# Pooled attention and two gated products on one core: probabilities transposed over 128 partitions, their blocks moved by transfers inside SBUF

## The chip, the cores and the metric

The kernel runs on one core of a Trainium2 chip. The metric is the device time of one execution in microseconds (us). Three runs of the kernel before took 1653.54, 1659.47 and 1664.84 us; their median is 1659.47 us. The engines are PE (TensorE), DVE (VectorE), ACT (ScalarE), POOL (GpSimd) and SP (SyncE, which here only issues transfers). All inputs are float32 arrays of the reference's shapes, except that the weights are held as 8-byte floats and are turned into 4-byte ones on the chip.

## The reference

```python
def _attn_ref(q, k, v):                       # B=8, H=8, S=576, D=64
    k_p = k.reshape(B, H, 72, 8, D).mean(axis=3)      # pooled by 8: 72 keys
    v_p = v.reshape(B, H, 72, 8, D).mean(axis=3)
    scores = np.matmul(q, k_p.transpose(0, 1, 3, 2)) / np.sqrt(D)
    scores = scores - np.max(scores, axis=-1, keepdims=True)
    attn = np.exp(scores)
    attn = attn / (np.sum(attn, axis=-1, keepdims=True) + 1e-09)
    return np.matmul(attn, v_p)

def _moe_ref(x, w1, w2, w3, w_out):           # x: 4608 x 512, d_ff 1024
    return ((x @ w1) * (x @ w2) @ w3) @ w_out

def _moe2_ref(x, w_gate, w_val, w_out, rms_g):    # d_ff 1536
    xn = x / np.sqrt(np.mean(x * x, axis=-1, keepdims=True) + 1e-06) * rms_g
    g = xn @ w_gate
    return (g * (1 / (1 + np.exp(-g))) * (xn @ w_val)) @ w_out
```

The attention's output of all heads, 512 columns for each of 4608 tokens, goes through the first product and then the second.

## The kernel before

The 4608 tokens are taken in nine blocks of 512 (`NB`), which do not fall together with the eight batches of 576. Matmuls are done on fp32r tiles split into a high and a low part, three matmuls for each product (`mm3`, lines 103 to 106), so that the times in the trace for lines L104, L105 and L106 are the kernel's main work.

The program has five stages:

1. Setup. w3 times w_out is formed on PE (L626), the weights w1 and w2 are converted (`Conv`), and batch 0 goes through attention.
2. The attention stage. For each block i, `ab(i, m, s)` (L564) makes one 128 x 512 piece of x @ w1 (s = 0) or x @ w2 (s = 1) in 12 matmuls, and their product h is stored to device memory (L575). Between these calls stand the steps of the next batch's attention, by a table of 16 positions for a block, `positions(i)` (L796): a position is the place after one `ab`.
3. The second stage, `second` (L489), multiplies the stored h, loaded again (`h_load`, L1185), with the formed w3 @ w_out. The result y of a block goes to device memory, and its mean square is formed on the way (`y_end`, L654: squares L659, the split L673, two matmuls with a column of ones L681 and L682, then small transfers L685, L687 and L692).
4. Block 0 of the second product (`gv`, L967).
5. The other eight blocks of it in pairs (`quad`, L1066).

The weights of stages 4 and 5 are prepared in twelve groups by `gv_steps` (L717): converted, combined by subtractions (L745), split (L100 on ACT, L101 on DVE) and stored by POOL (L762). Four groups are spread over stage 2 (`prep`), and eight, together with the conversion of the last weight w_o2 (`o2_jobs`, L861), over the end of stage 2 and the whole of stage 3 (`side`).

One batch's attention has five tiles of queries, four of 128 rows and one of 64. The steps of tile t are: `Q` (q is transposed on PE, L307, and copied by ACT, L312), `S` (scores on PE L325, row maximum on DVE L337, exponentials on ACT L340), `N` (division on DVE, L351 to L353), and `T` (the probabilities, rows = queries, are transposed so that rows = pooled keys, into the tile aT). For batches 0 and 1 `T` uses PE (L375) and ACT (L380). From batch 2 on it uses DVE's transpose of 32 x 32 blocks, each instruction on 32 partitions, straight into aT:

```python
for i in range(2 * hf, min(2 * hf + 2, n // 32)):
    for kb in range(SPP // 32):
        nc.vector.transpose(
            aT[32 * kb : 32 * kb + 32, :, s0 + 32 * i : s0 + 32 * i + 32],
            s_t[t][32 * i : 32 * i + 32, :, 32 * kb : 32 * kb + 32],
        )
```

`av_step` (L420) multiplies aT with the pooled v on PE (L428); ACT (L435) and DVE (L436) take the result out of PSUM as the high and low part of the next block's input. The first of `k0`, `k1`, `kT` load and pool k for the next batch (L247 from SP, L248 added by POOL) and transpose it on PE (L288).

A scheduler records each engine's instructions in one order, in which the engine runs them. Every transfer issued by SP or ACT counts its landing on one of eight semaphores (they are called DMAHW0 to DMAHW7), given out in turn, and waits before its issue for the landing of the transfer that had the same semaphore before it.

The attention's PSUM tiles (`pa`, `apsum`, L74) are four banks used in turn; a fifth use waits until the first has been read by ACT and DVE.

Of the kernel before, what the change touches and what calls it, by code (L numbers as in the profile page):

```python
# [21 lines left out]
def kernel(  # L22
# [17 lines left out]
    nc = tc.nc  # L40
# [223 lines left out]
    def att_steps(b):  # L264
        q_t, qT_t, s_t, mx_t, den_t, kv_t = {}, {}, {}, {}, {}, {}

        def load_q(g):
            if 2 * g >= NTL:
                return
            q_t[g] = at_p.tile([P, 2, H, D], F32, tag="q", name="q", bufs=2)  # L270
            for u, (s0, n) in enumerate(TILES[2 * g : 2 * g + 2]):
                nc.sync.dma_start(
                    out=q_t[g][:n, u], in_=q[b, :, s0 : s0 + n, :].rearrange("h s d -> s h d")
                )

# [18 lines left out]

        def step_Q(g, hf):
            if 2 * g >= NTL:
                return
            tiles = TILES[2 * g : 2 * g + 2]
            nu, n = len(tiles), tiles[0][1]
            qt = q_t[g].rearrange("s u h d -> s u (h d)")  # L300
            if hf == 0:
                qT_t[g] = at_p.tile([P, 2, NP, P], F32, tag="qT", name="qT", bufs=2)
            qT = qT_t[g]
            if hf < nu:
                ps = apsum()
                for p in range(NP):
                    nc.tensor.transpose(  # L307
                        ps[:, p * P : p * P + n],
                        qt[:n, hf, p * P : (p + 1) * P],
                        ident[:n, :n],  # L310
                    )
                nc.scalar.copy(  # L312
                    qT[:, hf, :, :n], ps.rearrange("d (p s) -> d p s", p=NP)[:, :, :n]
                )
            if hf == 1:
                q_t.pop(g)
                load_q(g + 2)

        def step_S(t, hf):
            s0, n = TILES[t]  # L320
            ps = apsum()
            if hf == 0:
                s_t[t] = sbuf[t % len(sbuf)]
            for p in (2 * hf, 2 * hf + 1):
                nc.tensor.matmul(  # L325
                    ps[:n, (p % 2) * 2 * SP : (p % 2 + 1) * 2 * SP],
                    qT_t[t // 2][:, t % 2, p, :n],
                    kT[:, p, :],
                    start=True,
                    stop=True,  # L330
                )
# [28 lines left out]
        def step_T(t, hf):  # L360
            s0, n = TILES[t]
            if t == 0 and hf == 0:
                st8["aT", b] = at_p.tile([SPP, H, S], F32, tag="aT", name="aT")
            aT = st8["aT", b]
            if b >= 2:
                for i in range(2 * hf, min(2 * hf + 2, n // 32)):
                    for kb in range(SPP // 32):
                        nc.vector.transpose(  # L368
                            aT[32 * kb : 32 * kb + 32, :, s0 + 32 * i : s0 + 32 * i + 32],
                            s_t[t][32 * i : 32 * i + 32, :, 32 * kb : 32 * kb + 32],  # L370
                        )
# [7 lines left out]
            dst = aT[:SP, 4 * hf : 4 * hf + 4, s0 : s0 + n]  # L379
            nc.scalar.copy(dst, src)  # L380

# [10 lines left out]
        def flat():  # L392
            steps = [step_kT, lambda: step_Q(0, 0), lambda: step_Q(0, 1)]
            for t in range(NTL):
# [6 lines left out]
                def e(t=t):  # L401
# [4 lines left out]
                    lambda t=t: step_S(t, 0),  # L406
                    lambda t=t: step_Q(t // 2 + 1, t % 2),
                    lambda t=t: step_S(t, 1),
                    d,
                    e,  # L410
# [4 lines left out]
        return SimpleNamespace(  # L415
            flat=flat, k0=step_k0, k1=step_k1, q=load_q, kT=step_kT, Q=step_Q,
            S=step_S, N=step_N, T=step_T, load_v=load_v, v=step_v,
        )

    def av_step(b, i, p):  # L420
# [143 lines left out]
    def ab(i, m, s):  # L564
# [152 lines left out]
    def gv_steps(G, s, kp):  # L717
        w = (w_gate, w_val)[s]
        cell = {}

        late = G > 0

# [64 lines left out]
    for n, (cs, steps) in enumerate(groups):  # L787
        gv_prep = preps[n >= 4]
        if n in (0, 4):
            gv_prep.append(lambda cs=cs: [cs_.s0() for cs_ in cs])  # L790
        if n + 1 not in (4, len(groups)):
            nxt = groups[n + 1][0]
            steps[4] = lambda f=steps[4], nxt=nxt: (nxt[0].s0(), nxt[1].s0(), f())
        gv_prep += steps

    def positions(i):  # L796
        pos = [[] for _ in range(2 * KF1)]
        b = i + 1
        if b >= B:
            return pos  # L800
        A = atts[b]
        pos[1] = av_steps(i, i + 1) + [
            lambda: A.S(0, 0), lambda: A.Q(1, 0), lambda: A.S(0, 1)
        ]
        pos[2] = [lambda: A.N(0)]
        for t in range(1, NTL):
            p = 2 * t + 1
            pos[p] += [lambda t=t: A.S(t, 0)]
            if t < 4:
                pos[p] += [lambda t=t: A.Q(1 + t // 2, t % 2)]  # L810
            pos[p] += [lambda t=t: A.S(t, 1)]
            pos[p + 1] += [
# [3 lines left out]
        pos[12] += [lambda: A.T(NTL - 1, 0), lambda: A.T(NTL - 1, 1)]  # L816
        pos[13] += av_steps(b, i + 1)
        if b + 1 < B:
# [4 lines left out]
            pos[11] += [C.k1, lambda: C.q(1)]  # L823
            pos[15] += [C.kT, lambda: C.Q(0, 0), lambda: C.Q(0, 1)]
        return pos
# [5 lines left out]
    pos = positions(0)  # L831
    pos[0] += [atts[1].kT, lambda: atts[1].Q(0, 0), lambda: atts[1].Q(0, 1)]
    half = [pos[2 * n] + pos[2 * n + 1] for n in range(KF1)]
# [504 lines left out]
```

## Time and profile before

| | us |
|---|---|
| median of three runs | 1659.47 |
| the profiled execution | 1663.74 |
| its span (first to last instruction) | 1662.0 |
| PE busy in the span | 1609.1 (97%) |
| DVE busy | 1018.0 (61%) |
| ACT busy | 680.1 (41%) |
| POOL busy | 93.1 (6%) |

A matmul's busy time overlaps that of the next one: a 128 x 512 matmul is shown as 389 ns long, while the next one starts some 227 ns after it. So PE's rate is read from counts in a stretch, and its losses from idle time and from the granted clock. The clock column is the share of full speed (2.4 GHz) that was granted; 0.5 is the lower of the two levels, 1.2 GHz. Times on the time axis are us from the start of the span.

### The profile page before, as it was taken

To read this page: it belongs to the slowest core of one execution; us is meant where nothing else is said; L and a number is where in the kernel's file an instruction comes from. 1 tells how busy PE (TensorE), PEld (TensorE's weight loads), DVE (VectorE), ACT (ScalarE), POOL (GpSimd) and SP (SyncE) were. 2 spreads that over 40 slices of the span, in tenths; PEclk is the share of its full clock that TensorE was granted. 3 is DMA by queue.
4 is the path that set the end of the run, shared out by engine and by line. 5 is a ranking of instruction groups with operands and counts; after the bars stand their busy time and mean duration, and the time that the engine had idled before them with its cause. 6 is when DMAs were issued, how large, how long until landed. Compare 5 with 4: busy or idle time off the path is not lost. (4 is left out here: it accounts for less than half of the span.)

```text
span 1662.0 us, 19939 instructions
## 1 busy us (share of the span) xinstructions
PE 1609.1 (97%) x7250; PEld 1281.7 (77%) x7250; DVE 1018.0 (61%) x1773; ACT 680.1 (41%) x1607; POOL 93.1 (6%) x107
## 2 busy tenths in 40 slices
PE   5899999999999999999899999999999999999999
PEld 2447778778777788888678888888888888888887
DVE  4677598779787147766736353485347635475444
ACT  4765635543453125555523233244323433233321
POOL 1001101110110011111000000000000000000000
PEclk9898999999999999999999999999999999999999
DMA  9858445664562178887887754467445735455422
GB/s 229 258 163 221 106 119 154 140 150 111 145 215 84 70 242 297 268 281 244 314 289 242 294 212 176 154 206 275 158 158 210 284 138 217 177 207 198 177 102 76
DMA packets 147462, 322.53 MB, mean 194 GB/s; under 512 B 52506, under 2 KB 79130, under 8 KB 129443
## 3 DMA queue, kind: packets, MB, share of 16 engines
q1 hardware_dynamic: 126210, 276.13, 49.2%
q0 software_dynamic: 21152, 45.12, 10.4%
q8 instruction: 57, 0.93, 0.2%
q14 instruction: 43, 0.34, 0.1%
HBM read 247.75 MB, written 73.44 MB: 193 GB/s over the span
## 5 line engine op out<-in xcount | busy, mean ns | idle before, releaser
L104 PE MATMUL ps<-xf,wr 128*128 128x512 f32 x576 | 224.1, 389 | 0.0
L106 PE MATMUL ps<-xf,wr 128*128 128x512 f32 x576 | 224.1, 389 | 0.0
L105 PE MATMUL ps<-xf,wr 128*128 128x512 f32 x576 | 224.1, 389 | 0.0
L105 PE MATMUL o<-ol,hch 128*128 128x512 f32 x384 | 149.4, 389 | 0.0
L104 PE MATMUL o<-oh,hch 128*128 128x512 f32 x384 | 149.4, 389 | 0.0
L106 PE MATMUL o<-oh,hcl 128*128 128x512 f32 x384 | 149.4, 389 | 0.0
L368 DVE STREAM_TRANSPOSE aT<-s 32x256 f32<-32x256 f32 x324 | 140.9, 435 | 5.2
L1081 ACT COPY f<-ps 128x512 f32<-128x512 f32 x144 | 84.4, 586 | 126.1 <-PE ps L106 121.3
L104 PEld LDWEIGHTS ps<-xf,wr 128*128 128x128 f32 x576 | 108.1, 188 | 22.6 <-ACT f L1081 0.2
L105 PEld LDWEIGHTS ps<-xf,wr 128*128 128x128 f32 x576 | 108.1, 188 | 22.4
L106 PEld LDWEIGHTS ps<-xf,wr 128*128 128x128 f32 x576 | 108.1, 188 | 22.4
L1085 DVE TENSOR_TENSOR f<-y,f 128x512 f32<-128x512 f32 x48 | 33.2, 691 | 149.9 <-PE y L106 149.9
L104 PE MATMUL ps<-xh,w1h 128*128 128x512 f32 x288 | 119.3, 414 | 0.0
L340 ACT ACTIVATE s<-pa,mx 128x72 f32<-128x72 f32 (+1 forms) x280 | 85.5, 332 | 73.8 <-DVE mx L337 73.7
L105 PE MATMUL ps<-xl,w1h 128*128 128x512 f32 x288 | 114.9, 399 | 0.0
L104 PE MATMUL ps<-xh,w2h 128*128 128x512 f32 x288 | 113.1, 393 | 1.8 <-ACT w2h L100 1.8
L106 PE MATMUL ps<-xh,w1l 128*128 128x512 f32 x288 | 113.7, 395 | 0.0
L106 PE MATMUL ps<-xh,w2l 128*128 128x512 f32 x288 | 112.4, 390 | 0.0
L105 PE MATMUL ps<-xl,w2h 128*128 128x512 f32 x288 | 112.4, 390 | 0.0
L1105 ACT CAST hch<-f 128x512 fp32r<-128x512 f32 x72 | 44.8, 623 | 105.0 <-DVE f L1099 105.0
L1167 DVE TENSOR_TENSOR acc<-o,acc 128x512 f32<-128x512 f32 x64 | 43.5, 687 | 68.1 <-PE o L106 68.1
L626 PE MATMUL wps<-wo,hl 128*128 128x512 f32 x128 | 68.9, 664 | 16.6 <-ACT hl L559 9.6
(198 smaller groups left out, 3253.9 us busy)
## 6 DMA issues: line engine op xcount, KB each, us to landing
wr<-wd SPq DMA_DIRECT2D x96, 1024.0 KB
wd<-wst POOLq DMA_DIRECT2D x48, 512.0 KB, 6.1
hr<-hd SPq DMA_DIRECT2D x36, 512.0 KB
oh<-od SPq DMA_DIRECT2D x15, 1024.0 KB
ol<-od SPq DMA_DIRECT2D x15, 1024.0 KB
wr<-wd SPq DMA_DIRECT2D x24, 512.0 KB
x1raw<-in_moe_w_dram SPq DMA_DIRECT2D x20, 512.0 KB
hd<-hh SPq DMA_DIRECT2D x40, 256.0 KB
```

Source lines behind the costliest of these rows:

```text
L104: nc.tensor.matmul(o, lh, rh, start=first, stop=False, skip_group_check=part)
L105: nc.tensor.matmul(o, lh, rl, start=False, stop=False, skip_group_check=part)
L106: nc.tensor.matmul(o, ll, rh, start=False, stop=last, skip_group_check=part)
L340: nc.scalar.activation(s_t[t][:n, h, :SP], pv[:, j, :], AF.Exp, bias=mx[:, j, :], accum_out=den_t[t][:n, h, :],)
L368: nc.vector.transpose(aT[32 * kb : 32 * kb + 32, :, s0 + 32 * i : s0 + 32 * i + 32], s_t[t][32 * i : 32 * i + 32, :, 32 * kb : 32 * kb + 32],)
L626: nc.tensor.matmul(wps[i], wt[:, i * P : (i + 1) * P], wo[j // 4][:, j % 4, :], start=j == 0, stop=j == KF1 - 1,)
L1081: nc.scalar.copy(t, bank)
L1085: nc.vector.tensor_tensor(out=t, in0=bank, in1=t, op=ALU.add)
L1105: nc.scalar.copy(hi, hf)
L1167: nc.vector.tensor_tensor(out=a, in0=ys[j], in1=a, op=ALU.add)
```

## The change

`T` of batches 2 to 7 becomes two parts. DVE transposes all partitions of a tile of queries at once, three instructions for a tile, into a new tile tT (two buffers); then SP issues transfers from SBUF to SBUF, one for each 32 x 32 block row, twelve for a tile of 128 queries and six for the tile of 64, which bring the blocks from the partitions of the queries to those of the keys in aT. aT is laid out anew, with 32 columns of a head side by side and the heads 32 columns apart, so `av_step` reads its operand in pieces of 32 columns, and ACT's copy of batches 0 and 1 (`T` on PE) writes in that layout.

q is loaded tile by tile into three buffers, and its transposes stand behind both halves of the scores instead of between them. h is stored from ACT's queue instead of SP's. Eight of the twelve weight groups instead of four are spread over stage 2. `av_steps` stands one position later.

```diff
-        def load_q(g):
-            if 2 * g >= NTL:
+        def load_q(t):
+            if t >= NTL:
                 return
-            q_t[g] = at_p.tile([P, 2, H, D], F32, tag="q", name="q", bufs=2)
-            for u, (s0, n) in enumerate(TILES[2 * g : 2 * g + 2]):
-                nc.sync.dma_start(
-                    out=q_t[g][:n, u], in_=q[b, :, s0 : s0 + n, :].rearrange("h s d -> s h d")
-                )
+            s0, n = TILES[t]
+            q_t[t] = at_p.tile([P, H, D], F32, tag="q", name="q", bufs=3)
+            nc.sync.dma_start(
+                out=q_t[t][:n], in_=q[b, :, s0 : s0 + n, :].rearrange("h s d -> s h d")
+            )
...
+            nc.scalar.copy(
+                qT_t[t][:, :, :n], ps.rearrange("d (p s) -> d p s", p=NP)[:, :, :n]
+            )
+            load_q(t + 3)
...
         def step_T(t, hf):
             s0, n = TILES[t]
+            g0, ng = s0 // 32, n // 32
             if t == 0 and hf == 0:
-                st8["aT", b] = at_p.tile([SPP, H, S], F32, tag="aT", name="aT")
+                st8["aT", b] = at_p.tile([SP, S // 32, H, 32], F32, tag="aT", name="aT")
             aT = st8["aT", b]
             if b >= 2:
-                for i in range(2 * hf, min(2 * hf + 2, n // 32)):
-                    for kb in range(SPP // 32):
-                        nc.vector.transpose(
-                            aT[32 * kb : 32 * kb + 32, :, s0 + 32 * i : s0 + 32 * i + 32],
-                            s_t[t][32 * i : 32 * i + 32, :, 32 * kb : 32 * kb + 32],
+                if hf:
+                    return
+                tT = at_p.tile([P, SPP // 32, H, 32], F32, tag="tT", name="tT", bufs=2)
+                for kb in range(SPP // 32):
+                    nc.vector.transpose(
+                        tT[:n, kb], s_t[t][:n, :, 32 * kb : 32 * kb + 32]
+                    )
+                for kb in range(SPP // 32):
+                    r = min(32, SP - 32 * kb)
+                    for i in range(ng):
+                        nc.sync.dma_start(
+                            out=aT[32 * kb : 32 * kb + r, g0 + i],
+                            in_=tT[32 * i : 32 * i + r, kb],
                         )
                 return
...
-                st8["aT", b][:SP, h, c0 : c0 + n],
+                st8["aT", b][:, c0 // 32 : (c0 + n) // 32, h, :],
...
-            h_put.append(lambda: nc.sync.dma_start(out=hdram[i][m], in_=hf))
+            h_put.append(lambda: nc.scalar.dma_start(out=hdram[i][m], in_=hf))
...
-        late = G > 0
+        late = G > 1
...
-        gv_prep = preps[n >= 4]
-        if n in (0, 4):
+        gv_prep = preps[n >= 8]
+        if n in (0, 8):
...
-            lambda: A.S(0, 0), lambda: A.Q(1, 0), lambda: A.S(0, 1)
+            lambda: A.S(0, 0), lambda: A.S(0, 1), lambda: A.Q(1)
...
-        pos[13] += av_steps(b, i + 1)
+        pos[14] += av_steps(b, i + 1)
```

What the scheduler makes of it is shown at three places. A name is a tile, `_121` and the like a buffer's number, `x3` three in a row.

The first place is DVE at the end of a block, from the last tile but one of the batch to the step that empties the banks `pa` of `av_step` (aT and tT: the transposes; den and s: the division; kv and vp: the pooling of k and v; xl: the banks being emptied). Before:

```order
L337 TENSOR_REDUCE mx<-pa 64x4
L368 STREAM_TRANSPOSE aT<-s_121 32x8x32 x11
L351 TENSOR_SCALAR den<-den 64x8
L574 TENSOR_TENSOR hh<-ps,f 128x512
L352 RECIPROCAL den<-den 64x8
L253 TENSOR_TENSOR kv<-kv 72x4x128
L353 TENSOR_TENSOR s_120<-s_120,den 64x8x72
...
L368 STREAM_TRANSPOSE aT<-s_120 32x8x32 x6
L574 TENSOR_TENSOR hl<-ps,f 128x512
L436 SCALAR_TENSOR_TENSOR xl_3173<-pa,xh_3172 128x192 x4
```

Of the change:

```order
L333 TENSOR_REDUCE mx<-pa 64x4 x2
L367 STREAM_TRANSPOSE tT<-s_121 128x256 x2
...
L349 TENSOR_TENSOR s_120<-s_120,den 64x8x72
L367 STREAM_TRANSPOSE tT<-s_120 64x256 x2
L581 TENSOR_TENSOR hh<-ps,f 128x512
...
L367 STREAM_TRANSPOSE tT<-s_120 64x256
...
L581 TENSOR_TENSOR hl<-ps,f 128x512
L443 SCALAR_TENSOR_TENSOR xl_3307<-pa,xh_3306 128x192
...
L443 SCALAR_TENSOR_TENSOR xl_3307<-pa,xh_3306 128x192 x3
```

Between the last maximum and the emptying of the banks 17 transposes of 32 partitions stood; now five of 128 or 64 partitions stand there.

The second place is SP's queue at two tiles of a batch in stage 2 (hd: h in device memory; in brackets the semaphores waited for). Before:

```order
L575 DMA hd_98<-hl 128x512 [waits DMAHW6_49,DVE_49]
L272 DMA q<-in_q_dram 128x8x64 [waits DMAHW7_49,PE_49]
L575 DMA hd_98<-hh 128x512 [waits DMAHW0_49,DVE_49]
L272 DMA q<-in_q_dram 128x8x64 [waits DMAHW1_49]
L272 DMA q<-in_q_dram 128x8x64 [waits DMAHW3_49,DMAHW2_49,PE_49]
L575 DMA hd_98<-hl 128x512 [waits DVE_49]
```

Of the change:

```order
L272 DMA q<-in_q_dram 128x8x64 [waits DMAHW1_49,PE_49]
L373 DMA aT<-tT 32x256 [waits DMAHW2_49,DVE_49]
L373 DMA aT<-tT 32x256 [waits DMAHW3_49]
L373 DMA aT<-tT 32x256 [waits DMAHW5_49]
L373 DMA aT<-tT 32x256 [waits DMAHW6_49]
L373 DMA aT<-tT 32x256 [waits DMAHW7_49,DVE_49]
L373 DMA aT<-tT 32x256 [waits DMAHW0_49]
L373 DMA aT<-tT 32x256 [waits DMAHW1_49]
L373 DMA aT<-tT 32x256 [waits DMAHW2_49]
L373 DMA aT<-tT 8x256 [waits DMAHW3_49,DVE_49]
L373 DMA aT<-tT 8x256 [waits DMAHW4_49]
L373 DMA aT<-tT 8x256 [waits DMAHW5_49]
```

The stores of h have left SP's queue, and the blocks of aT stand in it; from the eighth on each of them waits for the landing of one of the same tile. DMAHW4 is missing among the first because a store of h on ACT has it there.

The third place is ACT at the end of stage 3 (xq: w_o2 being converted; hb: h being split; of: w_o2 being split; `f<-y` and `hh<-y`: y of the last block but one; the last row is the split of its sum of squares, L673 before and L680 now). Before:

```order
L662 COPY hh<-y 128x512
L659 ACTIVATE f<-y 128x512 x2
L662 COPY hh<-y 128x512
L100 CAST hb<-hr 128x1024
L144 ACTIVATE xq<-xq 128x512
L147 ACTIVATE f<-xq 128x512
L673 CAST f<-f 128x512
```

Of the change:

```order
L669 COPY hh<-y 128x512
L666 ACTIVATE f<-y 128x512
L100 CAST hb<-hr 128x1024
L666 ACTIVATE f<-y 128x512
L669 COPY hh<-y 128x512
L100 CAST of<-of 128x2048
L680 CAST f<-f 128x512
```

The conversion step that stood in front of the split has moved; the split of a finished group of w_o2 stands there instead.

## Rows read from the trace of the kernel before

**Rows 1.** Busy time of each engine by stage (setup, attention, second stage, its end).

```profile
core 0: us, PE busy (x) PEld busy (x) DVE busy (x) ACT busy (x) POOL busy (x), PEclk, DMA share, GB/s
0.00:160.00 160.00, 128.01 (x471) 74.02 (x472) 99.41 (x192) 94.69 (x235) 15.64 (x22) 0.92 0.82 222
160.00:540.00 380.00, 374.02 (x1928) 298.55 (x1927) 314.57 (x710) 178.39 (x746) 38.55 (x38) 0.99 0.52 136
540.00:780.00 240.00, 240.00 (x1055) 194.54 (x1054) 136.40 (x200) 107.48 (x156) 30.77 (x37) 1.00 0.71 237
780.00:860.00 80.00, 68.83 (x282) 54.25 (x282) 46.84 (x67) 36.35 (x54) 7.10 (x9) 0.94 0.88 303
```

**Rows 2.** What PE waited for: us in total, times, longest us.

```profile
PE pa L288 <- DVE xl L436: 6.0, 4, 2.6
PE y L681 <- ACT f L673: 4.6, 1, 4.6
...
PE y L104 <- ACT f L684: 3.0, 1, 3.0
```

**Rows 3.** DVE from 197 to 540 us: busy, mean ns | idle before.

```profile
L368 DVE STREAM_TRANSPOSE aT<-s 32x256 f32<-32x256 f32 x324 | 140.9, 435 | 5.2
...
L353 DVE TENSOR_TENSOR s<-s,den 128x576 f32<-128x576 f32 x24 | 18.2, 757 | 0.7
...
L101 DVE TENSOR_TENSOR wst<-wf,wst 128x1024 fp32r<-128x1024 f32 x8 | 9.7, 1220 | 2.4 <-ACT wst L100 2.4
L745 DVE TENSOR_TENSOR wf<-wf 128x256 f32<-128x256 f32 x16 | 6.1, 417 | 0.1
L159 DVE SCALAR_TENSOR_TENSOR rawp<-rawp 128x512 int32<-128x512 int32 x8 | 5.5, 684 | 0.1
L171 DVE CUSTOM_DVE_ANT_0 wf<-rawp,f 128x1024 uint16<-128x1024 uint16 x8 | 5.4, 672 | 0.1
...
L353 DVE TENSOR_TENSOR s<-s,den 64x576 f32<-64x576 f32 x6 | 4.5, 748 | 0.1
...
L168 DVE TENSOR_SCALAR f<-f 128x512 int32<-128x512 int32 x8 | 3.4, 419 | 4.5 <-ACT f L147 4.5
```

**Rows 4.** DVE in order of time at one block's end: start, us.

```profile
415.45 2.67 DVE L368 STREAM_TRANSPOSE aT<-s 32x256 f32<-32x256 f32 x6
...
418.75 1.14 DVE L436 SCALAR_TENSOR_TENSOR xl<-pa,xh 128x192 fp32r<-128x192 f32 x4
```

**Rows 5.** PE in order of time at the same place.

```profile
419.16 0.47 PE L288 MATMUL pa<-ident,kv 72*128 72x72 f32 x4 [2.62 <-DVE xl L436]
```

**Rows 6.** Granted clock (third number from the right) behind two of PE's waits.

```profile
420.00:424.00 4.00, 4.00 (x14) 3.31 (x13) 2.76 (x3) 1.55 (x4) 1.98 (x3) 0.57 0.72 201
...
804.00:808.00 4.00, 3.38 (x8) 2.29 (x9) 3.41 (x5) 1.38 (x2) 0.00 (x0) 0.50 0.91 295
```

**Rows 7.** ACT in order of time at the end of the second stage.

```profile
802.72 0.65 ACT L144 ACTIVATE xq<-xq 128x512 int32<-128x512 uint32 x1 [3.01 <-DMA xq<-in_moe_w_out_dram]
...
803.83 0.61 ACT L673 CAST f<-f 128x512 fp32r<-128x512 f32 x1
```

**Rows 8.** What SP's queue waited for: us in total, times, longest us.

```profile
SPq L575 <- DVE hh L574: 127.7, 23, 10.6
...
SPq L687 <- DMA sdram<-f: 15.2, 7, 5.7
```

**Rows 9.** SP in order of time: a load of 288 KB, and a store of 2 KB.

```profile
404.02 0.35 SPq L247 DMA_DIRECT2D kv<-in_v_dram  x1
...
835.77 0.24 SPq L685 DMA_DIRECT2D sdram<-f  x1
...
844.50 0.32 SPq L687 DMA_DIRECT2D ss<-sdram  x1
```

**Rows 10.** POOL in order of time: the addition that waits for that load.

```profile
409.21 1.18 POOL L248 DMA_DIRECT2D kv<-in_v_dram  x1 [1.47 <-DMA kv<-in_v_dram]
```

**Rows 11.** The attention's last product on PE, the whole span: busy, mean ns.

```profile
L428 PE MATMUL pa<-aT,vp 72*64 72x64 f32 (+7 forms) x240 | 32.6, 406 | 2.7 <-ACT kT L293 2.7
```

More of the change, by code (lines that the diff above doesn't have):

```diff
@@ L265, in att_steps, with load_q3 @@
         q_t, qT_t, s_t, mx_t, den_t, kv_t = {}, {}, {}, {}, {}, {}
-        def load_q(g):
-            if 2 * g >= NTL:
+        def load_q(t):
+            if t >= NTL:
                 return
-            q_t[g] = at_p.tile([P, 2, H, D], F32, tag="q", name="q", bufs=2)
-            for u, (s0, n) in enumerate(TILES[2 * g : 2 * g + 2]):
-                nc.sync.dma_start(
-                    out=q_t[g][:n, u], in_=q[b, :, s0 : s0 + n, :].rearrange("h s d -> s h d")
-                )
+            s0, n = TILES[t]
[3 more added lines that the diff above has]
+            )
+        def load_q3(g):
+            for t in ((0, 1), (2,))[g]:
+                load_q(t)
         def step_k0():
@@ L293, in step_kT, with step_Q @@
             nc.scalar.activation(kT[D:, :, SP:], pv[D:], AF.Copy, scale=ATT_SCALE)
-        def step_Q(g, hf):
-            if 2 * g >= NTL:
+        def step_Q(t):
+            if t >= NTL:
                 return
[L298 to L313, printed above, removed]
-                )
-            if hf == 1:
-                q_t.pop(g)
-                load_q(g + 2)
+            n = TILES[t][1]
+            qt = q_t.pop(t).rearrange("s h d -> s (h d)")
+            qT_t[t] = at_p.tile([P, NP, P], F32, tag="qT", name="qT", bufs=2)
+            ps = apsum()
+            for p in range(NP):
+                nc.tensor.transpose(
+                    ps[:, p * P : p * P + n], qt[:n, p * P : (p + 1) * P], ident[:n, :n]
+                )
+            nc.scalar.copy(
+                qT_t[t][:, :, :n], ps.rearrange("d (p s) -> d p s", p=NP)[:, :, :n]
+            )
+            load_q(t + 3)
         def step_S(t, hf):
@@ L326, in step_S @@
                     ps[:n, (p % 2) * 2 * SP : (p % 2 + 1) * 2 * SP],
-                    qT_t[t // 2][:, t % 2, p, :n],
+                    qT_t[t][:, p, :n],
                     kT[:, p, :],
@@ L378, in step_T @@
             src = ps[:SP].rearrange("s (h t) -> s h t", h=4)[:, :, :n]
-            dst = aT[:SP, 4 * hf : 4 * hf + 4, s0 : s0 + n]
-            nc.scalar.copy(dst, src)
+            nc.scalar.copy(
+                aT[:, g0 : g0 + ng, 4 * hf : 4 * hf + 4, :],
+                src.rearrange("s h (g c) -> s g h c", c=32),
+            )
         def load_v():
@@ L392, in flat @@
         def flat():
-            steps = [step_kT, lambda: step_Q(0, 0), lambda: step_Q(0, 1)]
+            steps = [step_kT, lambda: step_Q(0)]
             for t in range(NTL):
@@ L406, in flat @@
                     lambda t=t: step_S(t, 0),
-                    lambda t=t: step_Q(t // 2 + 1, t % 2),
                     lambda t=t: step_S(t, 1),
+                    lambda t=t: step_Q(t + 1),
                     d,
@@ L415, in att_steps @@
         return SimpleNamespace(
-            flat=flat, k0=step_k0, k1=step_k1, q=load_q, kT=step_kT, Q=step_Q,
+            flat=flat, k0=step_k0, k1=step_k1, q=load_q3, kT=step_kT, Q=step_Q,
             S=step_S, N=step_N, T=step_T, load_v=load_v, v=step_v,
@@ L787 @@
     for n, (cs, steps) in enumerate(groups):
-        gv_prep = preps[n >= 4]
-        if n in (0, 4):
+        gv_prep = preps[n >= 8]
+        if n in (0, 8):
             gv_prep.append(lambda cs=cs: [cs_.s0() for cs_ in cs])
-        if n + 1 not in (4, len(groups)):
+        if n + 1 not in (8, len(groups)):
             nxt = groups[n + 1][0]
@@ L807, in positions @@
             p = 2 * t + 1
[L808 to L811, printed above, removed]
+            pos[p] += [lambda t=t: A.S(t, 0), lambda t=t: A.S(t, 1), lambda t=t: A.Q(t + 1)]
             pos[p + 1] += [
@@ L823, in positions @@
             pos[11] += [C.k1, lambda: C.q(1)]
-            pos[15] += [C.kT, lambda: C.Q(0, 0), lambda: C.Q(0, 1)]
+            pos[15] += [C.kT, lambda: C.Q(0)]
         return pos
@@ L831 @@
     pos = positions(0)
-    pos[0] += [atts[1].kT, lambda: atts[1].Q(0, 0), lambda: atts[1].Q(0, 1)]
+    pos[0] += [atts[1].kT, lambda: atts[1].Q(0)]
     half = [pos[2 * n] + pos[2 * n + 1] for n in range(KF1)]
```

## The prediction

> **What bounds the kernel now.** I began with busy time by stage. In the attention stage PE is busy 374.0 of 380 us, in the second stage all of it, at the end of the second stage 68.8 of 80, in the setup 128.0 of 160 [rows 1]. So PE is the bound, and a change can gain only what PE loses: 6.0 us of idle in the attention stage, 11.2 at the end of the second stage, 32 in the setup, and what the lower clock takes there (0.99, 0.94, 0.92 of full speed).
>
> Next, whom PE waits for. In the attention stage it is one wait: L288, the transposes of k at a block's end, stands four times, 6.0 us in all, for L436 on DVE, which empties the PSUM banks that L288 needs [rows 2]. DVE in order of time shows why L436 is late: six transposes stand before it until 418.1, it begins at 418.75, and PE goes on at 419.16 after 2.62 us of idle [rows 4, 5]. DVE is behind because of its load: its transposes are 324 times 435 ns, 140.9 us [rows 3]. Behind that wait the granted clock reads 0.57, the lower level for most of 4 us, after 1.00 before it [rows 6].
>
> At the end of the second stage PE waits 4.6 us for L673 and 3.0 us for L684, both on ACT [rows 2]. ACT is not busy there: at 802.72 it ends an idle time of 3.01 us with a conversion step whose load of w_o2 came late, and L673 stands in the queue behind it [rows 7]. The transfer engines are 0.88 busy in that stage, against 0.52 in the attention stage [rows 1].
>
> **The change, part by part.** *Transposes.* 324 become 90: three for each of five tiles of six batches. The price on 128 partitions isn't in the trace. From below it is 435 ns, the same 256 elements a partition; from above 4 x 435 = 1740 ns, if the four groups of 32 partitions went one after another. I take 435: L353 takes 757 ns on 128 partitions and 748 on 64, so DVE's time goes by elements per partition [rows 3]. DVE loses 234 x 435 = 101.8 us.
>
> The Trainium skill, "VectorE: DVE Perf Modes", section "The three transpose paths", has a 128 x 128 bf16 transpose done as a grid of independent 32 x 32 blocks in 311 ns. By it a 128 x 256 one would take about 622 ns, an estimate, and the loss would be 140.9 - 90 x 0.622 = 84.9 us, which leaves the sum as it is.
>
> *Weight groups.* Four more groups in the attention stage cost DVE 2 x (0.684 + 0.672 + 0.419 + 1.220) + 4 x 0.417 = 7.7 us each [rows 3], 30.7 in all. DVE's 314.6 us in that stage [rows 1] become 314.6 - 101.8 + 30.7 = 243.5, or 64% of 380 instead of 83%. Their loads and stores come along, 3 MB a group, 12 MB over 380 us, 32 GB/s beside 136 [rows 1].
>
> *The wait of L288.* Seventeen transposes stood between the last maximum and the emptying of the banks, 17 x 0.435 = 7.4 us; five stand there now, 2.2 us. The longest wait is 2.6 us [rows 2], so it should go, though `av_steps` moves one position nearer (12 matmuls, 12 x 240 / 1055 = 2.7 us, [rows 1]). That is 5.2 us less of DVE work against 2.7 us less of cover, a net 2.5 us at the longest wait, and DVE no longer arrives there late. Gain 6.0 us, and about 2 us of clock (4 us at 0.57 lose 1.7, the shorter waits a little): 8 us. From below the gain is nothing, if DVE still comes late.
>
> *Blocks of aT by transfer.* 324 new transfers, 54 a batch, at about 0.33 us of SP's time (0.35 and 0.32 for two others, [rows 9]): 18 us a block of some 57. They hide as long as aT is full when `av_step` comes. The last tile's are issued after position 12 and used after position 1 of the next block, five positions or 13.6 us later. A landing isn't in the trace for this size. From below it is 2.2 us, the mean of SP's wait for a 2 KB store (15.2 / 7, [rows 8]); from above 8.5, the one time that this store met full transfer engines (835.77 + 0.24 to 844.50, [rows 9]). The kv load in the attention stage landed within 5.2 us (404.02 to 409.21, [rows 9, 10]). I take 3, since 32 KB is nearer to the small store in the stage's half-idle engines. With eight semaphores a tile's last four wait for its first landings: 3 + 4 x 0.35 + 3 = 7.4 us after the first issue, inside 13.6. Cost 0.
>
> The Trainium skill, "DMA: Bandwidth & Descriptors", section "Anatomy of one DMA", speaks against many small transfers: each costs about 2 us whatever its size. One after another that would be 54 x 2 = 108 us a block, an estimate, and SP would bound the stage; eight at once it is 13.5 us. No row before shows which.
>
> *h from ACT's queue.* Eight stores a block leave SP, which stood 127.7 us for one of their kinds alone [rows 8]; q, k and v behind them go sooner, which nothing waits for. ACT gets 8 x 0.33 = 2.7 us a block and is 178.4 of 380 busy [rows 1]. A store there waits for a product that DVE made one `ab` earlier, and for its semaphore's last landing, usually a block of aT one tile before. Behind it stand the copies and exponentials; PE has three further banks, so I cost it at nothing. Without that cover each us of waiting is one of PE's.
>
> *Reading aT in pieces of 32 columns.* L428 is 32.6 us [rows 11]; no strided operand of PE stands in the trace. Between 0 and 32.6 I take 0: the pieces are contiguous and the count of columns is the same.
>
> *Order of q's transposes; the layout of ACT's copy; the setup.* The same instructions in another order; q's third and fourth loads wait for PE in SP's queue, one of them more than before. The setup loses 32 us [rows 1] in waits of single us, and I take 0 with 5 either way.
>
> *The end of the second stage.* `side` loses 32 of its 79 steps, so the steps of w_o2 (the last 14, with 12 loads of 512 KB and 6 stores of 1 MB) spread over some 25 of its 82 calls instead of 15. The conversion step in front of L673 is gone from ACT's queue there, and loads arrive sooner. I take the 4.6 us, a third of the 3.0, and 1.7 of clock (half of the 3.38 us that PE is busy at 0.50, [rows 6]): 7 us. From below 0 (the split of w_o2 that now stands ahead may be as late), from above all 11.2.
>
> **The sum.** 8 + 7 = 15 us off the profiled execution's 1663.74 gives 1648.7. That execution lies 4.3 above the median of the three runs; taking the gain from the median gives 1644.5. I say **1648**.
>
> **The rivals.** *Both gains, as forecast: 0.45*, 1640 to 1656. *Only the attention stage gains: 0.22.* For it: at the second stage's end PE also waits behind the chain of small transfers (L685, L687), which the change leaves in place [rows 9]. 1663.7 - 8 = 1655.7. *More than forecast: 0.13.* SP, freed of h, feeds the setup's last loads and the whole 11.2 us go: 1663.7 - 8 - 11.2 - 5 = 1639.5, down to 1630.
>
> *SP's queue takes the place of DVE, slower: 0.12.* A tile comes every two `ab`, 5.5 us plus its small matmuls, about 6.8. If a landing takes L, a full tile's twelve transfers hold SP for L + 1.4 us, and its q load 0.5 more. Over the four full tiles the delay is 4 x (L + 1.9 - 6.8), against a margin of 13.6 - L - 6 x 0.35 for the last tile's six. They meet at L = 6.2 us; above it `av_step` waits. At L = 7 the delay is 8.4 and the margin 4.5: 3.9 us a block and 1.7 of clock, six blocks, 34 us, so 1663.7 - 15 + 34 = 1683. For it: 8.5 us was seen, the kv load took 5.2. Against it: this stage's engines are at 0.52, and h has left the queue.
>
> *PE reads aT at half rate: 0.04.* 1648.7 + 32.6 = 1681. *The transposes cost fourfold, so DVE isn't relieved: 0.04.* 314.6 + 90 x 1.74 - 140.9 + 30.7 = 361 of 380: the waits at L288 stay or double, 1663.7 - 7 + 6 = 1663.
>
> **Range and chances.** 1% of the median is 16.6 us, about what a measurement of this kernel can tell from no change: below 1642.9 is faster, above 1676 slower. The forecast's lower part (0.17 of its 0.45, since from the median the same gain gives 1644.5) and 0.13 of more make faster 0.30; slower is 0.12 and 0.04 less a little for a mild queue, 0.14; the rest, 0.56, is the same. The range 1630 to 1670 holds the first three cases and the last.
>
> **What would show it.** Right: L288's wait on DVE gone from PE's list, the clock at 1.00 from 160 to 540 us; 90 transposes of some 0.44 us; DVE near 64% in that stage; SP's waits for L575 gone; L673's successor waiting under 1 us. Wrong: PE or DVE waiting for a transfer into aT, SP waiting for landings of aT, ACT idle before a store of h, L428's successor longer than 406 ns on average, or the same waits at the end of the second stage.

## The result and the profile after

The changed kernel takes 1675.01 us (median of 7 runs, 1669.74 to 1678.68) against 1662.23 us of the kernel before (7 runs): the ratio is 1.0079, 95% interval 1.0061 to 1.0097. It is 0.8% slower. The profiled execution took 1669.74 us, so the two profiles lie 6.0 us apart, less than the medians (12.8): it is the fastest of the seven, and in which stage the slower ones lose more, no run shows. Every time of a stage below comes from one profiled execution of its kernel.

The first step is to find the stage. The start of one and the same matmul in both traces tells it: the first of block 1, of block 7, of the second stage, of block 0 of the second product, and of the pairs.

| first matmul of | before | after | difference | gained or lost since the row above |
|---|---|---|---|---|
| block 1 | 191.43 | 178.05 | -13.38 | -13.4 |
| block 7 | 533.40 | 544.00 | +10.60 | **+24.0** |
| second stage | 625.40 | 636.00 | +10.60 | 0 |
| block 0 of the second product | 835.61 | 846.55 | +10.94 | +0.3 |
| the pairs | 937.29 | 942.25 | +4.96 | -6.0 |
| last instruction's end on PE | 1658.27 | 1664.03 | +5.76 | +0.8 |

So the attention stage (from block 1 to block 7, "the stage" from here on) went from 342.0 to 366.0 us, and the ends of the program gained. The windows that answer to [rows 1]:

```profile
0.00:160.00 160.00, 132.08 (x543) 79.61 (x544) 107.33 (x212) 106.15 (x290) 15.86 (x22) 0.98 0.83 226
160.00:540.00 380.00, 361.14 (x1799) 287.12 (x1798) 223.83 (x499) 179.09 (x707) 51.19 (x54) 0.97 0.67 176
540.00:780.00 240.00, 240.00 (x1066) 193.66 (x1065) 111.88 (x161) 92.28 (x138) 21.61 (x22) 1.00 0.60 199
780.00:860.00 80.00, 72.65 (x307) 58.50 (x306) 45.01 (x65) 36.14 (x54) 6.23 (x8) 0.94 0.87 313
```

DVE is relieved, 223.83 us instead of 314.57 (the forecast had 243.5), yet PE is busy 361.14 instead of 374.02, at a clock of 0.97 instead of 0.99. PE's waits, beside [rows 2]:

```profile
PE pa L292 <- DVE xl L443: 12.0, 4, 4.8
...
PE y L104 <- ACT f L691: 7.1, 1, 7.1
```

L292 (L288 before) waits four times as before, but 12.0 us instead of 6.0. DVE isn't the one that is late. One block's end shows it, in the order of time on PE, DVE and ACT, beside [rows 4, 5]:

```profile
413.66 1.52 PE L435 MATMUL pa<-aT,vp 72*64 72x192 f32 x16
422.88 0.53 PE L292 MATMUL pa<-ident,kv 72*128 72x72 f32 x4 [4.76 <-DVE xl L443]
```

```profile
415.35 0.69 DVE L581 TENSOR_TENSOR hl<-ps,f 128x512 f32<-128x512 f32 x1 [1.12 <-ACT f L578]
422.47 0.36 DVE L443 SCALAR_TENSOR_TENSOR xl<-pa,xh 128x192 fp32r<-128x192 f32 x1 [6.42 <-ACT xh L442]
```

```profile
414.37 0.33 ACTq L582 DMA_DIRECT2D hd<-hh  x1
414.73 0.59 ACT L578 COPY f<-ps 128x512 f32<-128x512 f32 x1 [5.35 <-PE pa L435]
421.19 0.33 ACTq L582 DMA_DIRECT2D hd<-hl  x1
421.62 0.59 ACT L578 COPY f<-ps 128x512 f32<-128x512 f32 x1 [6.30 <-DMA aT<-tT]
422.10 0.34 ACT L442 ACTIVATE xh<-pa 128x192 fp32r<-128x192 f32 x1
```

Read from the bottom up: ACT stands idle for 6.30 us in front of a store of h (421.19), until a block of aT has landed, though that store has nothing to do with aT: the transfer held the semaphore that the store takes. (That block's issue began at 415.26 and took 2.09 us; the last update of its semaphore came at 421.12.) Behind it in ACT's order stand the copies out of `pa`, and DVE's L443 waits 6.42 us for them. DVE had been done since 416.04, 6 us early. Behind PE's 4.76 us of idle the granted clock reads 0.64, between the two levels, as behind the waits in [rows 6]:

```profile
422.00:426.00 4.00, 2.77 (x12) 2.28 (x13) 3.31 (x8) 3.46 (x10) 0.00 (x0) 0.64 0.61 130
```

Over the whole kernel ACT loses 88 us in this way, one of the signs of being wrong that the prediction had named:

```profile
ACT s L336 <- DMA aT<-tT: 45.2, 8, 8.3
...
ACT f L578 <- DMA aT<-tT: 30.0, 5, 8.9
...
ACT wst L100 <- DMA aT<-tT: 12.8, 2, 6.7
```

Why the blocks come late stands in SP's order of time in the same block (357.7 to 424.5 us on PE), each row a run of transfers with the time from the first's start to the last's end:

```profile
377.06 8.85 SPq L373 DMA_DIRECT2D aT<-tT  x12
386.01 0.39 SPq L272 DMA_DIRECT2D q<-in_q_dram  x1
386.49 20.17 SPq L373 DMA_DIRECT2D aT<-tT  x24
406.76 0.39 SPq L272 DMA_DIRECT2D q<-in_q_dram  x1
407.26 0.55 SPq L373 DMA_DIRECT2D aT<-tT  x1
407.91 0.94 SPq L247 DMA_DIRECT2D kv<-in_v_dram  x2
408.91 10.59 SPq L373 DMA_DIRECT2D aT<-tT  x11
419.60 0.40 SPq L272 DMA_DIRECT2D q<-in_q_dram  x1
420.09 4.07 SPq L373 DMA_DIRECT2D aT<-tT  x6
```

All 54 transfers of a batch are here (12 + 24 + 1 + 11 + 6), with five loads between them, in 47.1 us; SP waited in it for only 3.0 us, in four places. The forecast had 18. By line, with their count and the minimum, median and maximum of one in ns:

```profile
L373 SPq DMA_DIRECT2D aT<-tT x324: 507/590/2700, 191.5 to 544.5; - x162
```

An issue takes SP 0.59 us, and 0.69 from start to start in the median, not the 0.32 to 0.35 of the nearest rows before [rows 9]. In the mean it is 0.72 and 0.81, since 45 of the 324 took over 0.9 us, 65 us together. Of these 45, 41 fell where the transfer engines were at least 0.8 busy. In the block above, the eight issues from 393.75 to 402.87 took 1.18 us in the median, with the transfer engines 0.85 busy; the eleven from 386.49 to 393.70 took 0.59, at 0.41. But the first four, from 377.06 on, took 0.57 to 0.59 at 1.00, so what stretches an issue isn't shown.

The rest of the forecast in the trace after: the transposes take 420 and 424 ns on 128 and 64 partitions, and reading aT in pieces of 32 columns costs nothing (406 ns in [rows 11]).

```profile
L367 DVE STREAM_TRANSPOSE tT<-s 128x256 f32<-128x256 f32 x69 | 26.5, 420 | 1.0 <-DMA aT<-tT 0.5
...
L367 DVE STREAM_TRANSPOSE tT<-s 64x256 f32<-64x256 f32 x18 | 7.4, 424 | 0.1
```

```profile
L435 PE MATMUL pa<-aT,vp 72*64 72x64 f32 (+7 forms) x240 | 32.4, 405 | 2.0 <-DMA aT<-tT 1.6 <-ACT kT L297 0.5
```

### The profile page after: what moved, and what is told of

Its sections match the earlier page's. It is cut to its first block, busy times and chain, and to the rows that moved or that the text cites. A ratio compares the mean times of both kernels' runs of the same rounds, so it can differ in the third digit from the quotient of the medians.

```text
span 1668.0 us, 20251 instructions
## 1 busy us (share of the span) xinstructions
PE 1609.4 (96%) x7250; PEld 1283.3 (77%) x7250; DVE 909.0 (54%) x1539; ACT 677.0 (41%) x1607; POOL 95.9 (6%) x107
## 4 chain that ended last, share of the span: by engine, by line
PE 68%; DMA 4%; issue 4%; DVE 2%; SPq 1%; ACT 1%; POOL 0%; ACTq 0%; DVEq 0%; POOLq 0%
PE ps L104 14%; PE ps L105 13%; PE ps L106 13%; PE o L104 5%; PE o L105 5%; PE o L106 5%; PE y L104 3%; PE y L105 3%; PE y L106 3%; DMA aT<-tT 2%; SPq L373 1%; PE pa L435 1%; DMA f<-rdram 1%; PE pa L321 1%; ACT s L336 1%
## 5 line engine op out<-in xcount | busy, mean ns | idle before, releaser
L1085 ACT COPY f<-ps 128x512 f32<-128x512 f32 x144 | 84.5, 587 | 125.4 <-PE ps L106 121.5
L578 ACT COPY f<-ps 128x512 f32<-128x512 f32 x72 | 43.2, 600 | 132.8 <-PE ps L106 61.0
L106 PEld LDWEIGHTS o<-oh,hcl 128*128 128x128 f32 x384 | 72.1, 188 | 15.0
L104 PEld LDWEIGHTS o<-oh,hch 128*128 128x128 f32 x384 | 72.1, 188 | 15.0
```

The lines of the kernel that those rows point to most:

```text
L104: nc.tensor.matmul(o, lh, rh, start=first, stop=False, skip_group_check=part)
L106: nc.tensor.matmul(o, ll, rh, start=False, stop=last, skip_group_check=part)
L578: nc.scalar.copy(a0[i, m], ps)
L1085: nc.scalar.copy(t, bank)
```

## The experiments

None leaves out a part of the computation; only places and routes of work differ. "Stage" is from the first matmul of block 1 to that of block 7.

| kernel | median us | ratio to before, 95% interval | stage us |
|---|---|---|---|
| before | 1660 to 1663 | 1 | 342.0 |
| changed | 1675.0 | 1.0061 to 1.0097 | 366.0 |
| h from SP | 1676.1 | 1.0053 to 1.0105 | 367.0 |
| h from POOL | 1686.0 | 1.0107 to 1.0164 | 366.0 |
| transposes straight into aT | 1670.2 | 1.0026 to 1.0062 | 361.6 |
| before, h from ACT | 1657.3 | 0.9950 to 0.9985 | 343.6 |
| changed, four groups | 1671.5 | 1.0046 to 1.0071 | 358.2 |
| straight into aT, four groups | 1667.4 | 1.0019 to 1.0040 | 351.9 |
| blocks through device memory | 1641.0 | 0.9857 to 0.9885 | 334.7 |
| the same, four groups | 1649.7 | 0.9909 to 0.9935 | 334.4 |
| blocks on two queues | 1641.0 | 0.9859 to 0.9913 | 334.5 |
| through memory, twelve loads | 1663.2 | 0.9996 to 1.0033 | 363.1 |
| through memory, h from SP | 1640.2 | 0.9854 to 0.9899 | 334.2 |
| order of q alone | 1655.4 | 0.9956 to 0.9981 | 338.4 |

**Is it ACT's queue?** My first theory took the trace at its word: the store of h blocks ACT. Two kernels take the stores off ACT.

```diff
-            h_put.append(lambda: nc.scalar.dma_start(out=hdram[i][m], in_=hf))
+            h_put.append(lambda: nc.sync.dma_start(out=hdram[i][m], in_=hf))
```

> The changed kernel with one line undone: h is stored from SP's queue again. Theory 1 (ACT's queue): the attention stage is longer because a store of h in ACT's in-order queue waits for the landing of the block of aT that had its semaphore before (88 us of ACT's waits), so the block's end on ACT and DVE is late. Then ACT's waits for aT go to under 5 us, PE's wait for L443 from 12.0 us to under 4, the stage from 366 us back to 340 to 346 and the total to 1648 to 1655. Theory 2 (late landings as such: the transfer engines are fuller, and the blocks of aT come late): the waits go from ACT to PE and DVE, the stage stays at 360 to 370 and the total at 1668 to 1678. Theory 3 (more weight work on DVE and ACT in the stage): no change either, with ACT idle and DVE late.

The second has `nc.gpsimd` in that place.

> The changed kernel with h stored from POOL's queue, whose transfers don't share the eight semaphores of SP's and ACT's. Theory 1: as with SP's queue or better, since SP keeps its order too: ACT's waits for aT gone, the stage 340 to 346 us, total 1646 to 1654. If a store stands behind one of POOL's own waits (it waits 93 us for split weights), the product's buffer comes free late and DVE waits for POOL at L581: the stage up to 355. Theory 2 or 3: 360 to 370, total 1668 to 1678.

Theory 1 fell. ACT's waits for aT are gone in both, and the stage stays at 367.0 and 366.0 us: PE now waits itself. First h from SP, then h from POOL:

```profile
PE pa L307 <- DMA q<-in_q_dram: 13.9, 3, 5.9
...
PE pa L435 <- DMA aT<-tT: 8.6, 4, 6.1
```

```profile
PE pa L435 <- DMA aT<-tT: 12.8, 2, 9.2
PE pa L435 <- DMA kv<-in_k_dram: 7.7, 2, 4.9
```

With h from POOL the stage is as long as with h from SP, but the median of 1686.0 us lies above what theory 2 said of the total; its profile is the fastest of its six executions (1678.6), and what the others lose besides, no run shows. PE's wait there also bounds a landing, on PE and then on SP (two issues that begin at 372.96 and 373.68; no later block of that batch follows them):

```profile
376.11 1.33 PE L435 MATMUL pa<-aT,vp 72*64 72x320 f32 x4 [4.87 <-DMA kv<-in_k_dram]
```

```profile
372.96 1.37 SPq L373 DMA_DIRECT2D aT<-tT  x2
```

The last block is issued at 373.68 (the queue's row ends at 374.33), and PE goes on at 376.11, 2.4 us later. The name in the bracket is that of another load, as the wait is for several semaphores. Over all 324 blocks of the changed kernel a landing took 2.15 us in the median, 3.0 in the mean and 8.4 at most, from the issue's start to the last update of the block's semaphore. The landing that the forecast took, 3 us, was of the right size; what is late is the issue.

**Is it T at all?** The next four kernels take T, the weight groups or all but the place of h back.

```diff
-                tT = at_p.tile([P, SPP // 32, H, 32], F32, tag="tT", name="tT", bufs=2)
...
+                for i in range(ng):
+                    for kb in range(SPP // 32):
+                        nc.vector.transpose(
+                            aT[32 * kb : 32 * kb + 32, g0 + i],
+                            s_t[t][32 * i : 32 * i + 32, :, 32 * kb : 32 * kb + 32],
+                        )
```

> The changed kernel with T as before: 324 transposes of 32 partitions straight into the new layout of aT, no tT and no blocks moved by transfers; h from ACT, eight weight groups, the later place of av_steps and the order of q stay. Theories 1 and 2: no aT transfer holds a semaphore or a transfer engine, so ACT's waits before the stores go to under 10 us and the stage to 342 to 352 us (DVE has about 100 us more, so L443 may wait as before or a little more); total 1650 to 1660. Theory 3: the stage stays above 360, total 1668 or more.

A miss for theories 1 and 2, and inside what theory 3 said: without any transfer into aT the stage is still 361.6 us. DVE, which has the old transposes and the four new weight groups, is the one that is late now, 324.92 us of 380, and L292's wait for it is 15.0:

```profile
160.00:540.00 380.00, 363.21 (x1841) 288.43 (x1840) 324.92 (x728) 180.95 (x721) 49.55 (x52) 0.98 0.57 155
```

So this kernel didn't tell the theories apart: it took one cause away and brought another. (Theory 3 falls for the changed kernel with the blocks through device memory, below: all eight groups, and a stage of 334.7 us.) The kernel before with h from ACT (the one line of above, the other way round) was cleaner.

> The kernel before with one line changed: h is stored from ACT's queue. Theory 1: a store there waits for the landing of a load of k, q, v or weights, most of them long done, so ACT's waits before L574's stores are under 15 us in the stage and the total is within 4 us of the kernel before (1655 to 1667). Rival (a store in ACT's queue costs by itself, whatever held its semaphore: it waits for DVE's product): 10 us or more slower than before.

As theory 1 expected of it (343.6 us in the stage, 1657.3 in all): a store of h in ACT's queue costs nothing where no late transfer has held its semaphore.

To separate blocks and weights, both were combined with four groups, and the blocks got a cheaper route.

```diff
-        late = G > 1
+        late = G > 0
...
-        gv_prep = preps[n >= 8]
+        gv_prep = preps[n >= 4]
```

> The changed kernel with four weight groups instead of eight in the attention stage, as before; the blocks of aT, h from ACT and the rest stay. Stage here: from the first matmul of block 1 to that of block 7, 342 us before, 366 changed. Theory A (SP's rate: a block of aT takes SP 0.68 us from start to start, twelve of them, a load of q and those of k and v more than a tile's 6.8 us, so the blocks are late whatever else is done): the stage stays at 358 to 366, total 1668 to 1678. Theory B (the four more weight groups cost by themselves: their steps stand in front of the block's end in ACT's and DVE's order, and their loads in SP's): the stage 344 to 350, total 1652 to 1660.

Measured 358.2 us in the stage, at the lower end of what theory A said; theory B alone is out. The four groups add 7.8 us to late blocks.

> The changed kernel with transposes straight into aT and four weight groups; h from ACT, the later place of av_steps and the order of q stay. With eight groups its stage took 361.6 us. Theory B: 342 to 347, total 1652 to 1660, near the kernel before with h from ACT (1657). Theory A says nothing of this kernel's stage except that no aT transfer is in it. Theory C (the later place of av_steps or the new order of q costs by itself): the stage stays over 352 and the total over 1664.

351.9 us, and 1667.4 in all, a miss for theory B: better by 9.7 without the groups, at the lower edge of theory C, and 8.3 worse than with h from ACT alone. The last run below takes that up.

**The blocks by another route.** Through device memory, four transfers a tile:

```diff
+    tdram = [
+        [dram_p.tile([P, 3, 256], F32, name=f"td{b}_{t}") for t in range(5)] for b in range(8)
+    ]
...
+                td = tdram[b][t]
+                nc.sync.dma_start(out=td[:n], in_=tT[:n].rearrange("p k h c -> p k (h c)"))
                 for kb in range(SPP // 32):
                     r = min(32, SP - 32 * kb)
-                    for i in range(ng):
-                        nc.sync.dma_start(
-                            out=aT[32 * kb : 32 * kb + r, g0 + i],
-                            in_=tT[32 * i : 32 * i + r, kb],
-                        )
+                    nc.sync.dma_start(
+                        out=aT[32 * kb : 32 * kb + r, g0 : g0 + ng].rearrange(
+                            "s i h c -> s i (h c)"
+                        ),
+                        in_=td[:n, kb].rearrange("(i s) x -> s i x", s=32)[:r],
+                    )
```

> The changed kernel with the blocks of aT moved by four transfers a tile instead of twelve: tT as a whole to device memory (one store), back into aT by three loads. Eight groups and h from ACT stay. Theory A: SP has 20 instead of 54 of them a block, a tile's four hold it under 5 us even with the wait for the store's landing, so ACT's waits for aT (88 us) fall under 20 and the stage to 343 to 350, total 1648 to 1656. Theory B: the stage stays at 358 to 364, total 1665 to 1674.

Theory A, and more than it said: 334.7 us in the stage, 1641.0 in all, 1.3% faster than the kernel before. The same bytes go twice through the transfer engines, which are 0.77 busy against 0.67 in the changed kernel, and PE has no wait left in the stage, at a clock of 1.00:

```profile
160.00:540.00 380.00, 379.88 (x1951) 302.03 (x1949) 233.09 (x514) 189.05 (x738) 50.88 (x54) 1.00 0.77 219
```

> As through memory, with four weight groups in the attention stage. Theory A: 343 to 348, total 1650 to 1658 (the end of the second stage as before). Theory B: 342 to 347, total 1650 to 1658. If both causes add (each takes about half of the 24 us), this one alone reaches 345, through memory with eight groups and the blocks with four both lie at 350 to 358.

334.4 us, below every range: where the blocks are not late, the four groups cost the stage 0.3 us, and they are worth 8.6 us of the median later on.

**Count, kind or queue?** That route changed the number, the kind and the size of the transfers at once. The next kernel changes one word: the transfers of 8 rows (18 of 54) come from POOL.

```diff
-                        nc.sync.dma_start(
+                        (nc.gpsimd if kb == 2 else nc.sync).dma_start(
                             out=aT[32 * kb : 32 * kb + r, g0 + i],
```

> The changed kernel with a third of the transfers into aT (those of 8 rows, 18 of 54 a block) issued from POOL instead of SP; number, kind and size of the transfers stay. Theory A as the rate of SP's queue: eight a tile at 0.68 us are 5.4 us and a load of q 0.5, under a tile's 6.8, so SP keeps up, ACT's waits for aT fall from 88 us to under 40 and the stage from 366 us to 340 to 350; total 1646 to 1658. Rival (it is the kind: a transfer from SBUF to SBUF lands late by itself, whoever issues it): the stage stays at 358 to 366, total 1666 to 1676.

334.5 us, 1641.0 in all: the same gain as through memory, with the number, kind and size of the transfers unchanged. Both are below theory A's ranges; ACT's waits for aT fall from 88 us to 16.2. So it is SP's queue, and the rival is out: the landings of SP's blocks are no shorter than in the changed kernel (3.05 us in the median, 3.6 in the mean), and PE waits nowhere in the stage. POOL's 18 blocks also leave the eight semaphores, but for landings at these SP's issues of blocks waited only 10.3 us in the whole stage of the changed kernel. An issue costs SP what it did, 0.588 us; there are a third fewer of them:

```profile
L373 SPq DMA_DIRECT2D aT<-tT x216: 507/588/3404, 193.2 to 505.0; - x108
L373 POOL DMA_DIRECT2D aT<-tT x108: 497/510/1277, 195.2 to 504.9; - x108
```

```profile
160.00:540.00 380.00, 380.00 (x1947) 301.74 (x1946) 231.52 (x512) 186.64 (x727) 106.70 (x162) 1.00 0.72 191
```

The Trainium skill, "DMA: Bandwidth & Descriptors", section "Rules for kernel authors", says that spreading transfers over several engines' queues brings no bandwidth and saves only issue time. Here that issue time was worth 34 us (1675.0 to 1641.0).

> As through memory, but with one load for each 32 x 32 block row as in the changed kernel: a store and twelve loads a tile instead of a store and three loads. If the number of issues is the cause: 13 x 0.35 to 0.6 us and 2 to 3 us of waiting for the store are 7 to 10 us a tile against 6.8; the stage 350 to 366 us, total 1655 to 1676, ACT waiting for aT again. If the kind (SBUF to SBUF) is the cause: the loads come from device memory as the three did, the stage stays at 334 to 340 and the total at 1640 to 1646. The trace gives the price of such an issue beside the 0.59 us of one from SBUF.

Thirteen issues a tile from SP, twelve of them loads from memory (`for i in range(ng)` around the load again): late as in the changed kernel, 363.1 us, ACT waits 30.7 us for aT and PE 6.6. An issue takes 0.42 us here for 32 rows and 0.29 for 8, and a tile's wait for its store comes on top, so the number of issues alone isn't tested by it:

```profile
398.85 14.57 SPq L378 DMA_DIRECT2D aT<-td  x23
...
419.72 9.83 SPq L378 DMA_DIRECT2D aT<-td  x18
```

> Through memory with h stored from SP's queue as in the kernel before. If ACT's in-order queue was a cause of its own: nothing to wait for there any more, the same total as through memory, 1639 to 1646. If SP's order matters (a store of h waits for DVE's product, 10.6 us at most in the kernel before, and the blocks of aT stand behind it): PE waits for aT at a few block ends, the stage 336 to 345 and the total 1642 to 1652.

The same as with h from ACT, 334.2 us: once SP has room, it doesn't matter whose queue h takes.

**The rest of the change.**

> Of the change only two things are left: q loaded tile by tile with its transposes behind the scores, and the layout of aT (written by DVE's direct transposes). h from SP, four groups, av_steps at its old place. Two questions. The setup: the first matmul of block 1 came 8 to 13 us earlier in every kernel with a part of the change, with h from ACT alone 10.7 us. If h from ACT gave it, it comes at 189 to 193 us here as before (191.4); if the order of q gives it as well, at 180 to 185. The stage: with these two, h from ACT and the later place of av_steps it took 351.9 us against 343.6 with h from ACT alone. If the order of q costs that, the stage is 349 to 354 and the total 1660 to 1672; if the later place does, 341 to 345 and the total 1652 to 1664.

The kernel is the one with transposes straight into aT and four groups, with h from SP and `pos[13]`. Its stage is 338.4 us, below both ranges and 3.6 less than before: the order of q doesn't cost. What cost 13.5 us in the kernel that it was made from (351.9) is the later place of `av_steps`, or that place together with h from ACT; the two weren't tried apart. Block 1 comes at 183.1, so the order of q gives 8 us in the setup by itself, h from ACT gave 10.7 by itself, and both together 8 to 13.

## Why the prediction was wrong

**The step that failed** is "Blocks of aT by transfer": "324 new transfers, 54 a batch, at about 0.33 us of SP's time ... Cost 0." The number of transfers held, and so did the landing (taken 3 us, measured 3.0 in the mean, and 2.3 to 3.4 from the last issue to PE's start in four waits with h from POOL); the cover of 13.6 us was not measured apart. The price of an issue did not hold: 0.59 us in the median, 0.69 from start to start, and 0.81 from start to start in the mean. I had taken it from loads of device memory [rows 9] and gave bounds for the landing but none for the issue, though no transfer inside SBUF stood in the trace. With the measured price the prediction's own sum gives a delay: a tile holds SP 12 x 0.69 + 0.5 = 8.8 us against its pace of 6.8, four tiles 7.9 us late; the cover left is 13.6 - 3 - 6 x 0.69 = 6.5, so 1.4 us a block are lost. With the mean of 0.81 it is 13.7 against 5.7, 8.0 us a block. Measured: the stage is 24.0 us longer than before, and 366.0 - 334.5 = 31.5 longer than with the blocks on two queues, which has the gain that was forecast for the stage: over six blocks 5.2 us each, the lower clock included, between the two. So the median price alone makes the blocks late. By this estimate the larger part of the loss comes from the lower clock, the stretched issues, the loads of k and v in the queue and SP's short waits; no run shows their shares apart.

**The rival "SP's queue takes the place of DVE"** (0.12, 3.9 us a block and 1.7 of clock if landings took 7 us) is what happened, in the queue that it named, by the issue instead of the landing. That its 5.6 us a block lie so near the measured 5.2 is luck: landings took 3.0 us in the mean, and the issues made up the rest. The Trainium skill, "DMA: Bandwidth & Descriptors", section "Anatomy of one DMA", has some 2 us for a small transfer whatever its size, fitted there for transfers issued from POOL. The landings from SP's queue, 2.15 us in the median, lie near it, but they were not the bound. Nearer is the Trainium skill, "Perfetto Trace Analysis", section "What 'DMA-bound' means", which has the issuing engine's sequencer as a bound of its own, seen as a solid row of issues. SP's 47.1 us, with 3.0 of waits in them, are nearly such a row, with the transfer engines 0.67 busy over the stage.

**h from ACT's queue, cost nothing**: half right. The store did block ACT, for 88 us, by the semaphore that I had named, and "three further banks" didn't cover that. But without late blocks it is free (343.6 and 334.7 us), and with them any other queue is as slow (367.0 and 366.0).

**The wait of L288, 8 us in the stage**: not in the changed kernel, but the term was sized well. With the blocks on two queues PE has no wait left in the stage, and it gains 342.0 - 334.5 = 7.5 us. DVE near 64% of the stage: measured 58.9% in the changed kernel and 60.9% there.

**The end of the second stage, 7 us**: near in size, wrong in place, and so luck. From the start of the second stage to that of the pairs it is 311.9 us before and 306.3 after, 5.6 less, but nothing at the end of the second stage. What is gained lies in block 0 of the second product, which the forecast didn't name: from its first matmul to that of the pairs it is 95.7 us in every kernel with eight groups and 101.7 to 105.3 in every kernel with four. L673's wait is gone, as forecast; the next one is longer. On DVE, on ACT and on PE in order of time:

```profile
818.18 1.90 DVE L942 TENSOR_TENSOR xr<-xr,f 128x512 f32<-128x512 f32 x3 [3.81 <-DMA f<-rdram]
```

```profile
818.91 1.95 ACT L945 ACTIVATE xnh<-xr,g_col 128x512 fp32r<-128x512 f32 x3 [6.40 <-DVE xr L942]
...
822.81 0.57 ACT L691 COPY f<-y 1x512 f32<-1x512 f32 x1
```

```profile
823.43 0.79 PE L104 MATMUL y<-hb,wp 128*128 128x512 f32 x1 [7.15 <-ACT f L691]
```

L691 stands behind L945, which waits through DVE for the small transfers of the row statistics (f<-rdram). That is the chain that the prediction gave to its second rival.

**The setup, 0 with 5 either way**: it gained 13.4 us in this pair of profiles, and 3.1 (h from POOL) to 11.7 (blocks on two queues) in the kernels of the experiments at the same matmul. Between the first matmuls of block 0 and block 1, 76.8 us before and 67.5 after, PE's clock was 0.93 before and 1.00 after, and with h from POOL it was 0.93 again, in 76.7 us. PE's longest waits in that stretch are 2.7 and 1.8 us before, 1.2 and 0.5 after, 3.9 and 1.5 with h from POOL, each time behind ACT. Two parts give most of the gain by themselves and don't add up; which of these waits goes with the lower clock is open.

**Transposes at 435 ns on 128 partitions, aT in pieces of 32 columns at no cost**: right (420 and 405 ns).

## What to carry to other kernels

A transfer has a price in the queue that issues it, apart from its bytes and its landing: count issues times that price against the pace at which the work comes, and take the price from a transfer of the same kind or bound it. Where an engine waits for a transfer that it doesn't use, the semaphore is the messenger: before moving the blocked instruction, look whether the transfer's own queue is a solid row. And try the parts of a change on a kernel in which no other part is in trouble: the four groups cost the stage 9.7, 7.8 or 0.3 us, depending on what else was late.

## What the runs showed that I had not expected

An issue's median price on SP goes with the kind of transfer: 0.59 us for 32 rows from SBUF to SBUF and 0.65 for 8 rows, 0.42 and 0.29 for the same rows from device memory; on ACT it was 0.33 for 128 rows of 2 KB to device memory. POOL took 0.51 us for the 8 rows. Why it is so, no run here shows. Nor does the price hold: most issues of over 0.9 us fell where the transfer engines were nearly full. And moving each block twice, through device memory with 20 issues a batch, was faster by 2% than once with 54.
